# First readers of loaded data pinned to their place, logits turned ahead of rows, two experts' weights spread over the last batch, and the overflow loop moved behind the last scatter

## The chip, the cores and the metric

The kernel runs on one core of a Trainium2 chip. The metric is device time in microseconds (us), the median of three runs. TensorE (PE) multiplies, VectorE (DVE) and ScalarE (ACT) work on tiles, GpSimd (POOL) issues the indirect DMAs, and SyncE (SP) issues the other DMAs.

## The reference

Squared-ReLU attention over 8 batches of 1856 rows, gated by `u`, and then a mixture of 16 experts (4 groups of 4) in which each of the 14,848 rows goes to one expert:

```python
scores = (1.0 / S) * np.matmul(z, z.transpose(0, 2, 1))
attn = np.maximum(scores, 0.0) ** 2
x = (u * np.matmul(attn, v)).reshape(B * S, D)       # D = 256
g_idx = np.argmax(x @ w_group, axis=1)               # 4 groups
...                                                  # g_w: softmax weight of the group
e_idx = np.argmax(xg @ w_expert[g], axis=1)          # 4 experts in the group, e_w likewise
h = np.maximum(xg[mask_e] @ w1[g, e], 0.0)           # 256 -> 1024
out[tok_idx] = (g_w * e_w)[:, None] * (h @ w2[g, e]) # 1024 -> 256
```

## The kernel before

**Attention.** Each batch is cut into four chunks of 512, 512, 416 and 416 query rows (c0 to c3), and each chunk into 15 key blocks: 480 steps, named (c, k) within a batch. A step issues the scores of the step five ahead (`scores(s + LEAD)`: two matmuls, a ReLU and a square on ACT, a high half `ah` and a low half `al` on DVE), and then six matmuls into the output (`attn_v`). Numbers are kept as a high and a low half in fp32r, so every operand that is loaded is split once: ACT copies the high half from the staging tile, and DVE subtracts to get the low half. These are the first readers of loaded data: `z2h` (L229), `vh` (L296), `w1h` (L173) and `w2` (L185).

**Routing.** After the last key block of a chunk, `chunk_end` makes `xT`. `planes` (ACT, L386) lays out its 16-bit planes, and four DMA transposes on SP (L392) turn them into rows. `logits` runs four matmuls (L400, L401), copies the result (ACT, L405), and one more DMA transpose on SP (L408) brings it to `lgx`; `logits_tr` (DVE, L414) is the first reader of `lgx`. Then `route` runs some 26 small DVE operations, three per step, and four indirect DMAs on POOL (L535) scatter the rows into one bucket per expert in DRAM.

**Order.** From step 15 to 479 the order on each engine is made by a planner. It simulates the program with a cost model and puts an instruction where its inputs are ready by that model; program order only decides between those that are ready. Each engine then runs its list strictly in order and waits at the head of it. The first 15 steps, and the whole expert stage (PE, ACT and DVE there), are in an order written by hand. `defer(s + n, ...)` sets after which step a piece is put into the program, `run_gens` advances `route`.

**The last batch (batch 7).** When the rows of batches 0 to 6 are counted, the experts are sorted by load. `fill` (POOL, L616) writes padding rows behind each expert's rows, 16 DMAs of 396 KB. The first expert's weights are loaded in four 512 KB pieces (`load_w`, L169 and L178) and split. The first 512 rows of the two fullest experts are already final; `load_rows(0)` and `load_rows(1)` fetch them, and `join_block` (L685 to L700) makes the operands of block 0.

**Experts.** 16 experts, most in two blocks of up to 512 rows; a block has eight steps g, each with six `up` and six `down` matmuls. The last chunk's deferred pieces and its `route` run in the first steps g. Results are turned back by DMA transposes (L760) and scattered to the output by POOL (L731). The last block's results come by `rows_down` without a transpose. At the end a loop (L1147) handles overflowing experts; with this data it runs no iteration.

Of the kernel before, what the change touches and what calls it, by code (L numbers as in the profile page):

```python
# [29 lines left out]
def tile_glu_attn_moe(  # L30
# [133 lines left out]

    def load_w(e, wt, piece, name):

        raw = new_stg(f"raw_{name}_{piece}")
        if piece < 2:
            nc.sync.dma_start(raw, w1[ds(e, 1), piece * P:(piece + 1) * P, :].rearrange("o p f -> p (o f)"))  # L169

            def split():
                hi, lo = wt["h"][piece], wt["l"][piece]
                nc.scalar.copy(out=hi, in_=raw)  # L173
                nc.vector.tensor_sub(out=lo, in0=raw, in1=f32(hi))
        else:
# [6 lines left out]
            def split():  # L182
                for j in range(2):
                    t = wt["2"][2 * q + j].rearrange("p (a t d) -> p a t d", a=2, t=2)
                    nc.scalar.copy(out=t[:, :, 0, :], in_=rv[:, 2 * j:2 * j + 2, :])  # L185
                    nc.vector.tensor_sub(out=t[:, :, 1, :], in0=rv[:, 2 * j:2 * j + 2, :], in1=f32(t[:, :, 0, :]))
# [3 lines left out]
    def new_w(name):  # L190
        h, l = [], []
        for d in range(ND):
            h.append(new_vb(f"w1h_{name}_{d}"))
            l.append(new_vb(f"w1l_{name}_{d}"))
        return {"h": h, "l": l, "2": [new_vb(f"w2_{name}_{q}") for q in range(4)]}
# [21 lines left out]
    def prep_z(b, c):  # L217
# [8 lines left out]
        def split():  # L226
            z2h = new_z(f"z2h_{b}_{c}")
            z2l = new_z(f"z2l_{b}_{c}")
            nc.scalar.copy(out=z2h[:, 0:wx], in_=zr[:, 0:wx])  # L229
# [49 lines left out]
    def prep_v(b, c):  # L279
# [12 lines left out]
        def split():  # L292
# [3 lines left out]
            nc.scalar.copy(out=vh[:, 0:e], in_=raw[:, 0:e])  # L296
# [59 lines left out]
    def chunk_end(s):  # L356
# [24 lines left out]
        def planes(d):  # L381
# [8 lines left out]
            if d == ND - 1:  # L390
                for t in range(nt):
                    nc.sync.dma_start_transpose(  # L392
                        rows[:, t, 0:D].bitcast(U16).rearrange("p (g d) -> p g d", d=P),
                        pl[:, t].rearrange("p g q -> p (g q)"),
                    )

# [15 lines left out]
        def logits_tr():  # L412
            lgf = rt_("lgf", [4, LP], f"{b}_{c}")[:, 0:nt]
            nc.vector.tensor_copy(  # L414
                out=lgf.bitcast(U16).rearrange("p t (l h) -> p t h l", h=2)[:, :, :, 0:2 * NL], in_=lgx[:, :, :, 0:2 * NL]
            )
# [26 lines left out]
    def route(b, c, rows, lg, nt, part):  # L443
# [25 lines left out]
        yield  # L469
        oh = t("oh", [NG, 4])  # L470
        nc.vector.tensor_tensor(out=oh, in0=key, in1=km.unsqueeze(2).to_broadcast([P, NG, 4]), op=ALU.is_equal)
        yield
# [12 lines left out]
        yield  # L485
        pre = t("pre", [nt, NE], BF16)
        nc.vector.tensor_copy(out=pre[:, 0, :], in_=oh16[:, 0, :])
        yield
        for i in range(1, nt):
            nc.vector.tensor_add(out=pre[:, i, :], in0=pre[:, i - 1, :], in1=oh16[:, i, :])  # L490
            yield
        yield True
        for _ in range(3):
            yield
# [14 lines left out]
        yield  # L509
        df = t("df", [nt])  # L510
# [4 lines left out]
        yield  # L515
        nc.vector.tensor_add(out=base, in0=pk[:, W:W + NE], in1=base)
        yield
        sm = t("sm", [NG])
        nc.vector.tensor_reduce(out=sm, in_=ex, axis=AX.X, op=ALU.add)
        yield  # L520
        nc.vector.tensor_scalar(out=sm, in0=sm, scalar1=1e-9, scalar2=None, op0=ALU.add)
        yield
        nc.vector.reciprocal(out=sm, in_=sm)
        yield
        smv = sm.rearrange("p (i g) -> p i g", g=5)
        sel = t("sel", [nt, 4])
        nc.vector.tensor_mul(out=sel, in0=smv[:, :, 1:5], in1=ohv[:, :, 0, :])
        yield
        ew = t("ew", [nt])
        nc.vector.tensor_reduce(out=ew, in_=sel, axis=AX.X, op=ALU.add)  # L530
        yield
        nc.vector.tensor_mul(out=rows[:, 0:nt, D].bitcast(F32), in0=ew, in1=smv[:, :, 0])
# [269 lines left out]
    PE, ACT, DVE, SP = (mybir.EngineType.PE, mybir.EngineType.Activation, mybir.EngineType.DVE, mybir.EngineType.SP)  # L802
# [65 lines left out]
    )  # L868
    xs = []
    e1_cuts = []  # L870
    def step(s):
        b, c, k = steps[s]
        nxt = s // NK + 1
        if k == 0:
            if nxt < B * NQ:
                load_ut(nxt // NQ, nxt % NQ)
            if b + 1 == B:
                if c == 0:
                    new_wt(0)
                pw.clear()  # L880
                if c:
                    pw.append(load_w(regs(0)[0], wts[0], c - 1, "e0"))
                if c == NQ - 1:
                    pw.append(load_w(regs(0)[0], wts[0], c, "e0"))
        if b + 1 == B and k in (11, 13) and pw:
            pw.pop(0)()
        if s == NS - 1:
            new_wt(1)
            e1_cuts.extend([load_w(regs(1)[0], wts[1], pc, "e1") for pc in range(2)])
# [10 lines left out]
        if b + 1 == B and c == NQ - 1 and k == 4:  # L900
            for i in range(NEARLY):
                load_rows(i)
        if s == NS - 4:
            xs.append(list(join_block(0))[-1])
        if b + 1 == B and 0 <= s - (NS - NQ * NK + NK + 1) < NE:
            fill(s - (NS - NQ * NK + NK + 1))
# [8 lines left out]
    pw = []  # L915
# [15 lines left out]
    def early(i):  # L931
        run_deferred(late["at"])
        run_gens(late["at"], 8)
# [135 lines left out]
    def weights_from(g):  # L1069
        i = g // NF  # L1070
        if i == 0:
            ld, cuts, when = 1, e1_cuts, (1, 2, 6, 8)
        else:
            pe_ = blocks[i - 1][0]
            ld = pe_ + 2 if last_use[pe_] == i - 1 and pe_ + 2 < NE else None
            when = (4, 7, 10, 13)
            if ld is None:
                return
            new_wt(ld)
            cuts = [load_w(regs(ld)[0], wts[ld], pc, f"e{ld}") for pc in range(2)]  # L1080
# [6 lines left out]
        for pc in range(4):  # L1087
            then(g + when[pc], lambda pc=pc: piece(pc))

    def downs(g):  # L1090
# [5 lines left out]
        if f == NF - 1:  # L1096
            for k, fn in enumerate(turn(i, yb.pop(i), rows_b.pop(i)[1], n)):
                then(g + AHEAD + 5 + k, fn)

    plans = []  # L1100
    order = tc.manual_schedule(
        engines={mybir.EngineType.PE, mybir.EngineType.Activation, mybir.EngineType.DVE}
    )
    with order:
        for g in range(NB * NF):
# [28 lines left out]
            if i >= OLD:  # L1134
# [5 lines left out]
                if i == NB - 1 and f == NF - 1:  # L1140
# [65 lines left out]
```

## Time and profile before

| | us |
|---|---|
| median of 3 runs (lowest, highest) | 1563.68 (1561.2, 1564.03) |
| the profiled execution, its own time | 1563.37 |
| its span | 1561.8 |
| PE busy in the span | 1529.6 |
| DVE busy | 1131.8 |
| ACT busy | 1004.3 |
| POOL busy | 307.6 |

The 1.6 us between span and own time lie outside the profiled instructions. A matmul's end is modelled, so PE counts as busy a little beyond its last start. The mean granted clock of the span was 0.994.

### The profile page before, as it was taken

The page shows a single profiled execution, that of the slowest core. Times are in us where ns is not written, and L with a number is a line of the kernel's source. Part 1 is how long each engine was busy: PE and PEld are TensorE (multiplying, and loading weights), DVE is VectorE, ACT ScalarE, POOL GpSimd, SP SyncE. Part 2 cuts the span into 40 slices and gives each one's busy share as a digit, 9 for nine tenths or more (in the row PEclk, how much of TensorE's full clock was granted, in tenths as well). Part 3 has the DMA queues.
Part 4 walks back from the last instruction along what each step waited for, and adds up shares of the span by engine and source line. Part 5 has one row for each costly group of instructions (what it writes and reads, how often), then busy time and mean ns, then how long its engine had stood idle before and what let it go on. Part 6 is the DMA issues. An engine that isn't in the chain of part 4 may idle for free.

```text
span 1561.8 us, 23340 instructions
## 1 busy us (share of the span) xinstructions
PE 1529.6 (98%) x7527; PEld 1337.7 (86%) x7527; DVE 1131.8 (72%) x2676; ACT 1004.3 (64%) x1896; POOL 307.6 (20%) x372
## 2 busy tenths in 40 slices
PE   9999999999999899999989999999999999999996
PEld 7897988978979889889869799998888888888895
DVE  7888787887897788887877668765665555666662
ACT  8887797887897787978867435444444444444441
POOL 0013111212112121212142221211211122221112
PEclk9999999999999999999999999999999999999998
DMA  4344252342433332413184454554444544544530
GB/s 140 102 100 98 64 137 56 80 115 67 106 83 79 106 87 56 112 46 101 51 267 100 101 117 118 131 132 107 115 122 113 129 118 124 125 125 126 127 78 27
DMA packets 297388, 163.52 MB, mean 105 GB/s; under 512 B 240027, under 2 KB 276899, under 8 KB 297264
## 3 DMA queue, kind: packets, MB, share of 16 engines
q1 hardware_dynamic: 283168, 124.24, 33.5%
q0 software_dynamic: 13744, 37.39, 7.6%
q8 instruction: 59, 0.97, 0.3%
q14 instruction: 65, 0.53, 0.1%
q10 hardware_dynamic: 352, 0.39, 0.1%
HBM read 72.50 MB, written 38.45 MB: 71 GB/s over the span
## 4 chain that ended last, share of the span: by engine, by line
issue 32%; PE 26%; DVE 6%; DMA 5%; POOL 5%; ACT 3%; SPq 1%; POOLq 0%; DVEq 0%; ACTq 0%
PE o L345 5%; PE o L346 5%; PE o L348 4%; POOL out_dram L731 4%; PE sc L315 2%; PE sc L316 2%; DMA lgx<-lgp 2%; DVE al L328 2%; DMA out_dram<-yf,meta 2%; PE ph L712 1%; PE ph L710 1%; PE ph L711 1%; DVE ah L325 1%; DMA raw_e<-in_w_dram 1%; PE y L728 1%
## 5 line engine op out<-in xcount | busy, mean ns | idle before, releaser
L715 ACT ACTIVATE hh<-ph 128x512 fp32r<-128x512 f32 (+10 forms) x288 | 156.3, 543 | 349.8 <-PE ph L712 336.1
L345 PE MATMUL o<-ah,vl 128*128 128x416 f32 (+1 forms) x960 | 359.0, 374 | 2.8 <-DVE ah L325 1.7
L346 PE MATMUL o<-ah,vh 128*128 128x416 f32 (+1 forms) x960 | 356.4, 371 | 0.0
L716 DVE SCALAR_TENSOR_TENSOR hl<-ph,hh 128x512 fp32r<-128x512 f32 (+10 forms) x288 | 177.3, 616 | 217.8 <-ACT hh L715 200.9
L318 ACT ACTIVATE r<-sc 128x512 f32<-128x512 f32 (+1 forms) x480 | 259.6, 553 | 104.9 <-PE sc L316 50.4
L328 DVE TENSOR_TENSOR al<-r,ah 128x512 fp32r<-128x512 f32 (+1 forms) x448 | 285.6, 638 | 31.6 <-ACT r L322 16.1
L348 PE MATMUL o<-al,vh 128*128 128x512 f32 (+1 forms) x896 | 290.4, 375 | 11.6 <-DVE al L328 10.7
L324 ACT ACTIVATE r<-r 128x512 f32<-128x512 f32 (+1 forms) x416 | 240.3, 591 | 5.8
L535 POOL DMA_INDIRECT bucket<-rows,di x128 | 141.2, 1103 | 449.7 <-issue 197.9
L731 POOL DMA_INDIRECT out_dram<-yf,meta x121 | 122.7, 1014 | 508.5 <-DVE yf L770 484.4
L712 PE MATMUL ph<-xl_m,w1h_e 128*128 128x512 f32 (+10 forms) x576 | 207.9, 361 | 1.2 <-issue 0.8
L710 PE MATMUL ph<-xh_m,w1l_e 128*128 128x512 f32 (+10 forms) x576 | 207.5, 360 | 0.4 <-DVE hl L716 0.4
L711 PE MATMUL ph<-xh_m,w1h_e 128*128 128x512 f32 (+10 forms) x576 | 207.6, 360 | 0.0
L345 PEld LDWEIGHTS o<-ah,vl 128*128 128x128 f32 x960 | 181.3, 189 | 25.9 <-DVE ah L325 4.1
L348 PEld LDWEIGHTS o<-al,vh 128*128 128x128 f32 x896 | 166.2, 189 | 38.9 <-DVE al L328 20.4
L346 PEld LDWEIGHTS o<-ah,vh 128*128 128x128 f32 x960 | 181.2, 189 | 18.9
L728 PE MATMUL y<-hl,w_e 128*128 128x512 f32 (+9 forms) x544 | 196.2, 361 | 0.0
L727 PE MATMUL y<-hh,w_e 128*128 128x512 f32 (+9 forms) x544 | 196.1, 360 | 0.0
L726 PE MATMUL y<-hh,w_e 128*128 128x512 f32 (+9 forms) x544 | 195.9, 360 | 0.0
L325 DVE CAST ah<-r 128x512 fp32r<-128x512 f32 (+1 forms) x416 | 169.4, 409 | 34.2 <-ACT r L324 27.5
L315 PE MATMUL sc<-zm,z2h 128*128 128x512 f32 (+1 forms) x480 | 181.7, 379 | 1.1 <-ACT r L318 1.0
L316 PE MATMUL sc<-zm,z2l 128*128 128x512 f32 (+1 forms) x480 | 178.6, 372 | 0.0
(171 smaller groups left out, 2102.2 us busy)
## 6 DMA issues: line engine op xcount, KB each, us to landing
raw_e<-in_w_dram SPq DMA_DIRECT2D x64, 512.0 KB
vr<-in_v_dram SPq DMA_DIRECT2D x23, 512.0 KB
ut<-in_uT_dram SPq DMA_DIRECT2D x16, 512.0 KB
ut<-in_uT_dram SPq DMA_DIRECT2D x16, 416.0 KB
bucket<-padrow POOLq DMA_DIRECT2D x16, 396.0 KB
zr<-in_zT_dram SPq DMA_DIRECT2D x47, 128.0 KB
vr<-in_v_dram SPq DMA_DIRECT2D x9, 256.0 KB
rows<-pl SPq DMA_TRANSPOSE x128
```

The source lines that it names most:

```text
L315: nc.tensor.matmul(ps[:, 0:w], z2h[:, ks], zm, start=True, stop=False)
L316: nc.tensor.matmul(ps[:, 0:w], z2l[:, ks], zm, start=False, stop=True)
L318: nc.scalar.activation(out=a, in_=ps[:, 0:w], func=AF.Relu, scale=1.0 / S)
L324: nc.scalar.activation(out=a, in_=a, func=AF.Square)
L328: nc.vector.tensor_sub(out=al, in0=a, in1=f32(ah))
L345: nc.tensor.matmul(o, vl[:, dsl], ah, start=(k == 0), stop=False)
L346: nc.tensor.matmul(o, vh[:, dsl], ah, start=False, stop=(k == NK - 1))
L348: nc.tensor.matmul(o, vh[:, dsl], al, start=False, stop=False)
L710: nc.tensor.matmul(o, wt["l"][d][:, fs], xh[:, d, 0:W], start=(d == 0), stop=False)
L711: nc.tensor.matmul(o, wt["h"][d][:, fs], xh[:, d, 0:W], start=False, stop=False)
L712: nc.tensor.matmul(o, wt["h"][d][:, fs], xl[:, d, 0:W], start=False, stop=(d == ND - 1))
L728: nc.tensor.matmul(o, w2t[:, 0, dsl], hl_[:, 0:W], start=False, stop=(f == NF - 1))
```

## The change

- **Pins.** `held` ties an instruction behind whatever was put into the program before it on its engine, so that the planner can't move it ahead. It is used for the ACT copies that read loaded data first, for `logits_tr` on DVE, and for the four row transposes on SP.
- **Logits ahead of rows.** `logits` at step s + 2 now precedes `planes` at s + 3 and s + 4 (before: `planes` at s + 1 and s + 2, `logits` at s + 2). `logits_tr` comes at s + 6 instead of s + 8. For the last chunk it is the other way: `logits` at s + 5 (before s + 3), `logits_tr` at s + 8 (before s + 6), and `route` then runs up to 20 operations a step instead of 8.
- **Route.** The softmax weights are computed between the other operations, ahead of the scatter address.
- **Last batch.** The first expert's four weight pieces are loaded at (1,4), (1,5), (1,10), (1,14) and split at (1,9), (1,13), (2,5), (2,8); before, their loads were put at the starts of c1, c2 and c3. The second expert's pieces are loaded in c2 and c3, and three of them split there; before, all four were split in the expert stage. The fills go two per step from (1,5), instead of one per step from (1,1). `load_rows(0)` is at (2,3) and `load_rows(1)` at (3,4), before both at (3,4); block 0 is joined at (2,10) to (2,12), before at (3,11).
- **Expert stage.** SP is in hand order there too. Rows go out one step later.
- **The end.** The last block's `rows_down` and the overflow loop are in one hand order for all engines, POOL too, so the loop's instructions come behind the last scatter.

```diff
+    free = [True]
+
+    def held(ins):
+        if free:
+            tc.keep_in_program_order(ins)
...
-                nc.scalar.copy(out=hi, in_=raw)
+                held(nc.scalar.copy(out=hi, in_=raw))
...
-                    tr = nc.sync.dma_start_transpose(
+                    if s >= NHELD:
+                        held(tr)
...
-        defer(s + 1, lambda: planes(0))
-        defer(s + 2, lambda: planes(1))
-        defer(s + (3 if last else 2), logits)
-        wait = 6 if last else 8
+        defer(s + (5 if last else 2), logits)
+        defer(s + 3, lambda: planes(0))
+        defer(s + 4, lambda: planes(1))
+        wait = 8 if last else 6
         defer(s + wait, logits_tr)
-        gens.append((max(s + wait + 1, 42), g))
+        gens.append((s + wait if last else max(s + wait + 1, 42), g))
...
+    E0_LOADS = ((1, 4), (1, 5), (1, 10), (1, 14))
+    E0_CUTS = ((1, 9), (1, 13), (2, 5), (2, 8))
+    E1_LOADS = ((2, 9), (2, 13), (3, 7), (3, 11))
+    E1_CUTS = ((3, 6), (3, 9), (3, 13))
+    X0_LOADS = ((2, 3), (3, 4))
+    X0_JOINS = ((2, 10), (2, 11), (2, 12))
...
-        if b + 1 == B and 0 <= s - (NS - NQ * NK + NK + 1) < NE:
-            fill(s - (NS - NQ * NK + NK + 1))
+        if b + 1 == B and c == 1 and 5 <= k < 5 + NE // 2:
+            for e in range(2 * (k - 5), 2 * (k - 5) + 2):
+                fill(e)
...
-        run_gens(late["at"], 8)
+        run_gens(late["at"], 20)
...
-        engines={mybir.EngineType.PE, mybir.EngineType.Activation, mybir.EngineType.DVE}
+        engines={PE, ACT, DVE, SP}
...
+        with tc.manual_schedule(engines={POOL}):
+            for t in range((n + P - 1) // P):
+                rows_down(i, wts[e], hs, rows_b[i][1], n, t, next_view)
+            assert not hb
+            overflow()
```

## Rows read from the trace of the kernel before

**Rows 1.** The page, parts 1 and 2: busy time by engine, and the granted clock by slices.

```profile
PE 1529.6 (98%) x7527; PEld 1337.7 (86%) x7527; DVE 1131.8 (72%) x2676; ACT 1004.3 (64%) x1896; POOL 307.6 (20%) x372
PEclk9999999999999999999999999999999999999998
```

**Rows 2.** Waits of all engines (us in total, times, longest us).

```profile
DVE lgf L414 <- DMA lgx<-lgp: 62.6, 31, 5.0
...
PE o L348 <- DVE al L328: 10.7, 9, 4.0
...
ACT w1h_e L173 <- DMA raw_e<-in_w_dram: 5.9, 2, 4.4
...
ACT w_e L185 <- DMA raw_e<-in_w_dram: 2.9, 1, 2.9
```

**Rows 3.** Stretches: busy PE, PEld, DVE, ACT, POOL, then PEclk, DMA share, GB/s.

```profile
120.00:140.00 20.00, 17.95 (x72) 13.36 (x71) 14.86 (x50) 14.04 (x28) 6.54 (x9) 0.91 0.63 113
320.00:340.00 20.00, 18.68 (x83) 14.64 (x84) 19.34 (x55) 17.63 (x35) 2.91 (x4) 1.00 0.51 139
530.00:550.00 20.00, 15.17 (x61) 13.03 (x62) 17.41 (x49) 13.93 (x27) 0.64 (x2) 0.83 0.45 115
700.00:750.00 50.00, 50.00 (x266) 47.66 (x265) 40.38 (x122) 41.37 (x86) 9.41 (x13) 1.00 0.31 81
790.00:830.00 40.00, 35.45 (x164) 28.97 (x163) 28.93 (x79) 27.17 (x53) 13.14 (x20) 1.00 0.73 231
815.00:862.00 47.00, 44.42 (x227) 40.31 (x226) 37.14 (x115) 33.73 (x70) 10.18 (x13) 1.00 0.41 105
850.00:870.00 20.00, 17.66 (x83) 14.39 (x82) 16.02 (x46) 10.67 (x20) 4.67 (x6) 1.00 0.54 133
900.00:910.00 10.00, 9.22 (x46) 7.91 (x45) 6.28 (x10) 4.25 (x8) 4.35 (x4) 1.00 0.34 83
950.00:1500.00 550.00, 550.00 (x2720) 481.64 (x2719) 346.27 (x531) 252.75 (x453) 105.44 (x110) 1.00 0.49 122
```

**Rows 4.** Timeline of DVE from 126.6 us (start, us, what).

```profile
130.09 0.46 DVE L414 COPY lgf<-lgx 128x320 uint16<-128x320 uint16 x1 [3.42 <-DMA lgx<-lgp]
```

**Rows 5.** Timeline of SP and DVE ahead of 530 us.

```profile
523.95 0.57 SPq L284 DMA_DIRECT2D vr<-in_v_dram  x1
...
524.63 1.19 SPq L408 DMA_TRANSPOSE lgx<-lgp  x1
```

**Rows 6.** Timeline of all engines from 530.7 us.

```profile
530.76 0.35 DVE L414 COPY lgf<-lgx 128x320 uint16<-128x320 uint16 x1 [5.03 <-DMA lgx<-lgp]
...
533.82 0.71 PE L348 MATMUL o<-al,vh 128*128 128x416 f32 x1 [4.02 <-DVE al L328]
```

**Rows 7.** Timeline of PE from 529.3 us.

```profile
529.41 0.39 PE L316 MATMUL sc<-zm,z2l 128*128 128x512 f32 x1
```

**Rows 8.** The chain of waits, 785 to 815 us (start, us, what).

```profile
787.11 4.33 DMA raw_e<-in_w_dram
...
797.51 11.67 DMA raw_e<-in_w_dram
```

**Rows 9.** Line L616, the fills: min/median/max ns, first and last start.

```profile
L616 POOL DMA_DIRECT2D bucket<-padrow x16: 727/727/798, 778.6 to 806.3; - x16
```

**Rows 10.** Groups on DVE, 780 to 905 us (busy, mean ns, idle before).

```profile
L186 DVE TENSOR_TENSOR w_e<-raw_e,w_e 128x512 fp32r<-128x512 f32 x8 | 5.3, 686 | 1.5 <-ACT w_e L185 1.5
L174 DVE TENSOR_TENSOR w1l_e<-raw_e,w1h_e 128x1024 fp32r<-128x1024 f32 x4 | 4.9, 1224 | 3.3 <-ACT w1h_e L173 2.9 <-issue 0.4
...
L465 DVE TENSOR_TENSOR key<-key,iota 128x80 f32<-128x80 f32 x4 | 1.0, 240 | 0.1
```

**Rows 11.** Timeline of all engines from 1550.3 us.

```profile
1550.34 0.48 DVE L794 SCALAR_TENSOR_TENSOR y<-py,meta,tm 96x256 f32<-96x256 f32 x1 [2.33 <-ACT tm L793]
1553.11 0.92 POOL L731 DMA_INDIRECT out_dram<-y,meta  x1 [3.84 <-issue]
```

**Rows 12.** Line L1202, the end of the program.

```profile
L1202 POOLq DRAIN  x3: 40/115/8015, 1552.9 to 1561.5; - x3
```

More of the change, by code (lines that the diff above doesn't have):

```diff
@@ L190, in new_w, with add_w @@
     def new_w(name):
[L191 to L195, printed above, removed]
+        wt = {"h": [], "l": [], "2": []}
+        for piece in range(4):
+            add_w(wt, piece, name)
+        return wt
+    def add_w(wt, piece, name):
+        if piece < 2:
+            wt["h"].append(new_vb(f"w1h_{name}_{piece}"))
+            wt["l"].append(new_vb(f"w1l_{name}_{piece}"))
+        else:
+            wt["2"] += [new_vb(f"w2_{name}_{2 * (piece - 2) + j}") for j in range(2)]
     def new_wt(e):
@@ L491, in route @@
             yield
+            if i == 1:
+                sel = t("sel", [nt, 4])
+                nc.vector.tensor_mul(out=sel, in0=smv[:, :, 1:5], in1=ohv[:, :, 0, :])
+                yield
+            elif i == 2:
+                ew = t("ew", [nt])
+                nc.vector.tensor_reduce(out=ew, in_=sel, axis=AX.X, op=ALU.add)
+                yield
+        nc.vector.tensor_mul(out=rows[:, 0:nt, D].bitcast(F32), in0=ew, in1=smv[:, :, 0])
         yield True
-        for _ in range(3):
-            yield
+        yield
         pk = bank(ps_m, "m", f"pk_{b}_{c}")
@@ L800, in next_view @@
         return oviews[ocnt[0] - 1]
-    PE, ACT, DVE, SP = (mybir.EngineType.PE, mybir.EngineType.Activation, mybir.EngineType.DVE, mybir.EngineType.SP)
+    PE, ACT, DVE, SP, POOL = (
+        mybir.EngineType.PE, mybir.EngineType.Activation, mybir.EngineType.DVE, mybir.EngineType.SP, mybir.EngineType.Pool
+    )
     def first_batch():
@@ L879, in step @@
                     new_wt(0)
[L880 to L889, printed above, removed]
+        if b + 1 == B:
+            if (c, k) in E0_LOADS:
+                e0_cuts.append(load_w(regs(0)[0], wts[0], E0_LOADS.index((c, k)), "e0"))
+            if (c, k) in E0_CUTS:
+                e0_cuts[E0_CUTS.index((c, k))]()
+            if (c, k) in E1_LOADS:
+                wts.setdefault(1, {"h": [], "l": [], "2": []})
+                e1_cuts.append(load_w(regs(1)[0], wts[1], E1_LOADS.index((c, k)), "e1"))
+            if (c, k) in E1_CUTS:
+                pc = E1_CUTS.index((c, k))
+                add_w(wts[1], pc, "e1")
+                e1_cuts[pc]()
+            if (c, k) in X0_LOADS:
+                load_rows(X0_LOADS.index((c, k)))
+            if (c, k) == X0_JOINS[0]:
+                x0.append(join_block(0))
+            if (c, k) in X0_JOINS:
+                xs[:] = [next(x0[0])]
         if b + 1 < B:
@@ L1071, in weights_from, with last_piece @@
         if i == 0:
[L1072 to L1080, printed above, removed]
+            def last_piece():
+                add_w(wts[1], 3, "e1")
+                e1_cuts[3]()
+            then(g + 5, last_piece)
+            return
+        pe_ = blocks[i - 1][0]
+        ld = pe_ + 2 if last_use[pe_] == i - 1 and pe_ + 2 < NE else None
+        if ld is None:
+            return
+        new_wt(ld)
+        cuts = [load_w(regs(ld)[0], wts[ld], pc, f"e{ld}") for pc in range(2)]
         def piece(pc):
@@ L1087, in weights_from @@
         for pc in range(4):
-            then(g + when[pc], lambda pc=pc: piece(pc))
+            then(g + (4, 7, 10, 13)[pc], lambda pc=pc: piece(pc))
     def downs(g):
```

109 lines of the change are left out of this document (49 added, 60 removed).

## The prediction, made before the changed kernel was run

> **What bounds the kernel now.** The page comes first: PE is busy for 1529.6 of 1561.8 us [rows 1]. So PE sets the time, and only two things can be gained: what PE stands idle or runs at the lower clock, and what lies behind its last matmul. The view of stretches comes next, to find where PE stands. In the expert stage there is nothing: from 950 to 1500 us PE is busy for 550 of 550 us [rows 3]. The losses sit in six short stretches. In attention they are 120 to 140 us (17.95 of 20 busy), 320 to 340 (18.68) and 530 to 550 (15.17); around the last batch they are 790 to 830 (35.45 of 40), 850 to 870 (17.66 of 20) and 900 to 910 (9.22 of 10) [rows 3]. Idle time adds up to 2.05 + 1.32 + 4.83 = 8.2 us in the first three and 4.55 + 2.34 + 0.78 = 7.7 us in the last three. In two of them the granted clock is down as well, 0.91 and 0.83 [rows 3]: PE stood still, and then ran for some microseconds at the lower of its levels.
>
> The view of waits tells who is late. PE waits for `al` of DVE (10.7 us in 9 waits). DVE in turn waits 62.6 us in 31 waits for `lgx`, the transposed logits, and ACT waits 5.9 + 2.9 us for weights [rows 2]. The timeline joins the two. At 530.76 DVE begins to read `lgx` after 5.03 us of standing, and the `al` behind it releases PE at 533.82, after 4.02 us [rows 6]; PE's last start before was at 529.41 [rows 7]. The planner had put the reader where its model has `lgx` landed, and DVE's list is strictly in order. Most of the 31 waits cost PE nothing, because DVE works ahead; the 3.42 us wait at 130.09 [rows 4] and the 5.03 us one outlast that lead.
>
> **The change part by part.**
>
> *Logits first, reader pinned.* Before, four row transposes were put on SP's list ahead of that of the logits, and a `v` load could stand there too: the one at 523.95 preceded the logits' transpose at 524.63, which landed only by 530.76 [rows 5, 6]. Now the four come behind, and the reader can't stand ahead of the DVE work of step s + 11 (it is put into the program after `scores(s + 6 + LEAD)`). DVE can be at most those five steps ahead of PE, so the reader runs no earlier than six steps after the chunk's end. A step of 416 columns is 8 matmuls; 266 of them took 50 us from 700 to 750 [rows 3], so a step is 1.5 us and the place at least 9 us behind, later if DVE has less lead. I expect most of the 62.6 us of waits to go. What they cost PE in batches 0 to 6 is 8.2 us idle, plus the clock: (1 - 0.91) x 20 = 1.8 us, and (1 - 0.83) x 20 = 3.4 us, of which I count 2.0, since part of that low clock fell into the idle time. That is 12.0 us. A load may still stand ahead of a logits transpose, as the one at 523.95 did, so I take 80%: **-9.6 us**. Bounds: 0 (the reader is early again) and -13.
>
> *Hidden idle.* At 533.82 the page's idle is 4.02 us, but from 529.41 to 533.82 are 4.41 us between starts, and a 416-column matmul needs 0.19 (50 / 266): 0.2 us more was lost than the idle time shows. With some two dozen gaps in the six stretches I take **-2.5 us**, bounds 0 and -5.
>
> *Last batch.* The chain of waits shows one weight load landing in 4.33 us and the one at 797.51 in 11.67 us [rows 8]; the 16 fills run from 778.6 to 806.3 us [rows 9], and ACT stood behind those loads. Now each split is 5, 8, 10 and 9 steps behind its load: at 1.8 us a step in c1 the shortest is 9 us, the others 13 us or more, over the 11.67 us. The first load goes out a step before the fills, so it should land like the 4.33 us one. `load_rows(0)` and the join of block 0 move a chunk earlier, away from the wait for `xp` and the last logits. Against this, three more pieces are split in c3: a w1 piece costs DVE 1.22 us, a w2 piece twice 0.69 us [rows 10], together 3.8 us. DVE was busy for 37.14 of 47 us from 815 to 862 [rows 3], so it rises to 40.9, which is 92% of the 44.4 us that PE worked there. That just fits, not without small waits. Of 7.7 us I take 75%: **-5.8 us**, bounds -1 and -7.7.
>
> One page speaks against this part. The row: 11.67 us for a weight load beside the fills, 231 GB/s as a mean over that stretch [rows 3, 8]. The Trainium skill, page "DMA: Bandwidth & Descriptors", section "Issuing engines are not separate DMA queues", says that DMAs issued by different engines end up on the same 16 DMA engines and interleave; the trace agrees. By that rule the loads at (1,4) and (1,5), with the fills from (1,5), still share: should the first take 11.67 us, ACT would stand for 11.67 - 9 = 2.7 us at its split, and the sum would be some 2 us worse.
>
> *Last chunk's route.* `logits`, `logits_tr` and `route` stand two steps g later, but up to 20 operations go at once. A small DVE operation costs 0.24 us [rows 10], so 17 of them are a burst of 4 us, and the position matmuls that follow stand on PE's list behind it. **+1.0 us**, bounds 0 and +2.5.
>
> *SP by hand in the expert stage: 0.* SP's list waits there for ACT and DVE work of the same step g, and a weight piece is split at least three steps (8 us) after its load is put in. The cover is PE's 550 of 550 us. If it went, each block start could lose what 900 to 910 lost, 0.78 us [rows 3]. `route`'s reorder and the other pins: the same instructions, hidden behind PE in attention: 0.
>
> *The end.* The last `y` is written at 1550.82, its scatter starts only at 1553.11 [rows 11], because the loop's instructions stand ahead of it on POOL. That scatter can be 2.0 us earlier, but the loop's instructions now come behind it, and POOL's closing drain, which began at 1552.9, took 8.0 us [rows 12]. If the drain counts from the scatter: -2.0. If it counts from its own start: POOL stood 3.84 us between its last two scatters [rows 11], and those instructions come on top, some +1 to +3 us. No row decides; I take **0**, bounds -2 and +3.
>
> Sum: -9.6 - 2.5 - 5.8 + 1.0 + 0 = -16.9 us. Against the profiled execution's 1563.4 us (the median of the runs is 1563.7, so the same within 0.3) that is **1547 us**.
>
> **The rivals.**
>
> *Last batch bound by DVE and ACT.* If 92% of DVE can't be kept in order, c2 and c3 lose what they gain: 1547 + 4 = 1551. For: 40.38 of 50 is the fullest steady stretch of attention without loss [rows 3]. Against: the other batches' `v` and `z` splits are absent.
>
> *Half given back.* Pins fix a few instructions; the planner orders the rest anew, and the gaps return elsewhere: 1547 + 8 = 1555.
>
> *The pins change nothing for `lgx`.* With a load ahead on SP the transposed logits still land behind the pinned place, and only the last batch gains: 1547 + 9.6 = 1557.
>
> *Slower: the pinned reader is early in chunk after chunk.* A pin can't be moved back by the planner. The 3.42 us wait cost PE 2.05 us idle and 1.8 us of clock in its stretch [rows 3, 4], some 3.8 us. If seven more chunks of the 32 do that, the gain on the logits is gone and 27 us come on top: 1557 + 27 = 1584. It decides from about two more chunks on. Against: the place is at least 9 us behind, and SP no longer has the rows first.
>
> **How the numbers follow.** The forecast has 0.54, the last batch bound 0.14, half given back 0.12, no gain on `lgx` 0.09, the slower case 0.09, and 0.02 remain for a larger gain. A change under 0.2% (3 us) can't be told from none. Of the 0.09 without gain on `lgx` I give 0.04 to no change, and 0.01 of the half given back. Faster: 0.86, no change 0.05, slower 0.09. The low end takes the better bounds of the logits, hidden idle and the end together (-3.4 - 2.5 - 2, and the last batch in full): 1547 - 10 = 1537, with a little room 1536; the high end takes in the third rival with the end's +3: 1560.
>
> **What would show it.** `lgx` waits on DVE fall from 62.6 us to below 15, and ACT's waits for weights to zero. The dips of the granted clock near 130 and 530 us vanish. PE's idle time from 120 to 910 us falls below 6 us. The last scatter starts right behind the last `y`. Wrong: new waits of DVE or ACT right at the pinned readers, or PE waits in c2 and c3 of the last batch.

## Result, and the profile after

The changed kernel takes 1541.8 us, the median of four runs (1540.96 to 1543.94), against 1563.48 us beside it (1561.2 to 1564.03): a ratio of 0.9866, with a 95% interval of 0.9849 to 0.9883. It is faster, by 5 us more than forecast and inside the range. Executions of one kernel differ by some us, so two medians 2 to 3 us apart are only told apart where their intervals are. The profiled execution has an own time of 1542.55 us and a span of 1540.9 us.

The page first: PE's busy time, and the head of the chain that ended last (the work that led to the end, followed back step by step). It runs mostly through matmuls.

```profile
PE 1518.9 (99%) x7527; PEld 1336.9 (87%) x7527; DVE 1117.9 (73%) x2676; ACT 1000.0 (65%) x1896; POOL 307.6 (20%) x372
...
PE 48%; issue 3%; DVE 2%; DMA 2%; ACT 1%; SPq 1%; POOL 1%; POOLq 0%; DVEq 0%; ACTq 0%
```

The waits of all engines (us in total, times, longest) answer to [rows 2]: `lgx` costs DVE 18.4 us instead of 62.6, PE's waits for `al` have gone from 10.7 us to 0.4, and ACT's two waits for weights are as long as they were.

```profile
DVE lgf L428 <- DMA lgx<-lgp: 18.4, 13, 3.0
...
ACT w1h_e L179 <- DMA raw_e<-in_w_dram: 5.9, 1, 5.9
...
ACT w_e L191 <- DMA raw_e<-in_w_dram: 3.0, 1, 3.0
...
PE o L360 <- DVE al L340: 0.4, 1, 0.4
```

The same stretches as in [rows 3], and 15 to 700 us, which is batches 0 to 6 but for their edges; there the kernel before has PE busy for 675.00 us, with 3214 matmuls. All three dips of attention are gone, 20.00 of 20 at a clock of 1.00. Around the last batch a loss remains, and 790 to 830 us has a lower clock than before.

```profile
15.00:700.00 685.00, 684.60 (x3315) 602.60 (x3314) 566.08 (x1605) 573.35 (x1102) 124.30 (x150) 1.00 0.35 91
120.00:140.00 20.00, 20.00 (x93) 16.22 (x92) 17.81 (x52) 15.47 (x29) 6.46 (x8) 1.00 0.40 108
320.00:340.00 20.00, 20.00 (x92) 16.24 (x91) 15.80 (x40) 16.77 (x33) 4.90 (x5) 1.00 0.40 107
530.00:550.00 20.00, 20.00 (x91) 16.54 (x91) 16.91 (x49) 16.48 (x30) 4.66 (x5) 1.00 0.31 81
790.00:830.00 40.00, 37.38 (x187) 34.43 (x188) 33.15 (x95) 34.29 (x71) 7.06 (x11) 0.96 0.50 154
815.00:862.00 47.00, 45.30 (x219) 38.73 (x218) 40.02 (x120) 29.78 (x62) 10.96 (x12) 1.00 0.53 122
850.00:870.00 20.00, 19.24 (x87) 15.51 (x86) 12.31 (x39) 10.60 (x20) 8.21 (x8) 1.00 0.40 81
900.00:910.00 10.00, 10.00 (x68) 10.00 (x67) 7.42 (x16) 4.47 (x11) 4.15 (x4) 1.00 0.35 93
```

Where the time came from is read from three marks in the timelines: the first `xT` of batch 0's third chunk (88.73 us before, 88.77 after), the first `xT` of batch 6's last chunk, and the last `y`. The second mark, before and then after:

```profile
750.07 1.08 DVE L366 TENSOR_TENSOR xT<-o,ut 128x416 f32<-128x416 f32 x2
```

```profile
730.78 0.58 DVE L378 TENSOR_TENSOR xT<-o,ut 128x416 f32<-128x416 f32 x1
```

So batches 0 to 6 gave 19.3 us. The last `y` ends at 1528.95 instead of 1550.82 [rows 11], 21.9 us earlier, so the last batch and the experts gave 2.6 in these two executions. From there to the end of the span are 12.0 us instead of 10.9, which takes about 1 back (all timelines count from the span's start).

The view of stretches between the first two marks, before and then after, holds the same work but for four matmuls. PE's idle time falls from 10.00 to 0.40 us, which is half of the gain; the other half is busy time, 651.34 against 641.61.

```profile
88.73:750.07 661.34, 651.34 (x3132) 568.91 (x3131) 540.12 (x1548) 537.50 (x1039) 130.52 (x155) 0.99 0.36 88
```

```profile
88.77:730.78 642.01, 641.61 (x3128) 567.06 (x3127) 528.73 (x1544) 533.41 (x1039) 128.77 (x155) 1.00 0.35 90
```

How a turned logits transpose now looks, from the timelines of SP and DVE in batch 1, at the place of [rows 4]: it goes out at 121.56, the four row transposes behind it, and `lgf` reads at 125.33 without any wait.

```profile
121.56 1.21 SPq L422 DMA_TRANSPOSE lgx<-lgp  x1
123.36 5.29 SPq L404 DMA_TRANSPOSE rows<-pl  x4
...
125.33 0.35 DVE L428 COPY lgf<-lgx 128x320 uint16<-128x320 uint16 x1
```

What remains in the last batch is in the chain of waits from 770 us. Four row transposes take 2.58 to 3.23 us each (without the fills beside them 1.28, below), the load of the first expert's second piece stands behind them on SP until 782.77, and then takes 7.27 us to land.

```profile
770.73 2.58 SPq L404
...
773.36 2.91 SPq L404
...
776.32 2.97 SPq L404
...
779.34 3.23 SPq L404 DMA_TRANSPOSE rows<-pl  x1
...
782.77 7.27 DMA raw_e<-in_w_dram
```

The timelines of ACT and PE show what that costs: ACT's split, pinned ahead of the next ReLU, stands 5.92 us, PE stands 3.26 us for that ReLU, and behind it matmuls of 416 columns appear with 0.55 us instead of 0.35.

```profile
790.07 1.04 ACT L179 CAST w1h_e<-raw_e 128x1024 fp32r<-128x1024 f32 x1 [5.92 <-DMA raw_e<-in_w_dram]
...
791.59 0.45 PE L327 MATMUL sc<-zm,z2h 128*128 128x416 f32 x1 [3.26 <-ACT r L330]
...
792.44 0.35 PE L357 MATMUL o<-ah,vl 128*128 128x416 f32 x1
792.63 0.55 PE L327 MATMUL sc<-zm,z2h 128*128 128x416 f32 x1
```

The last chunk's `route`: PE waits at its position matmuls (`pk`), 0.21 + 0.53 us.

```profile
861.35 0.20 PE L529 MATMUL pk<-oh,tri 128*128 128x64 bf16 x1 [0.21 <-DVE oh L503]
862.08 0.18 PE L530 MATMUL pk<-pre,ones 128*128 128x48 bf16 x1 [0.53 <-DVE pre L512]
```

The end: the last scatter starts 0.28 us behind the last `y`, and POOL's closing drain (the third number is the longest, in ns) begins at 1533.2 and lasts 6.85 us.

```profile
1528.47 0.48 DVE L808 SCALAR_TENSOR_TENSOR y<-py,meta,tm 96x256 f32<-96x256 f32 x1 [2.33 <-ACT tm L807]
1529.23 0.92 POOL L745 DMA_INDIRECT out_dram<-y,meta  x1 [1.83 <-DVE y L808]
...
L1239 POOLq DRAIN  x3: 40/109/6854, 1533.2 to 1540.7; - x3
```

### The profile page after: what moved, and what is told of

Its sections match the earlier page's. It is cut to its first block, busy times and chain, and to the rows that moved or that the text cites. A ratio compares the mean times of both kernels' runs of the same rounds, so it can differ in the third digit from the quotient of the medians.

```text
span 1540.9 us, 23215 instructions
## 1 busy us (share of the span) xinstructions
PE 1518.9 (99%) x7527; PEld 1336.9 (87%) x7527; DVE 1117.9 (73%) x2676; ACT 1000.0 (65%) x1896; POOL 307.6 (20%) x372
## 4 chain that ended last, share of the span: by engine, by line
PE 48%; issue 3%; DVE 2%; DMA 2%; ACT 1%; SPq 1%; POOL 1%; POOLq 0%; DVEq 0%; ACTq 0%
PE ph L726 7%; PE ph L725 7%; PE ph L724 7%; PE y L742 6%; PE y L741 6%; PE y L740 6%; PE o L357 2%; PE o L358 2%; PE o L360 2%; PE sc L327 1%; PE sc L328 1%; PE py L802 1%; DMA raw_e<-in_w_dram 1%; SPq L404 1%; POOL out_dram L745 0%
## 5 line engine op out<-in xcount | busy, mean ns | idle before, releaser
L357 PE MATMUL o<-ah,vl 128*128 128x512 f32 (+1 forms) x960 | 357.0, 373 | 1.6 <-DVE ah L337 1.4
L358 PE MATMUL o<-ah,vh 128*128 128x512 f32 (+1 forms) x960 | 356.7, 372 | 0.0
L360 PE MATMUL o<-al,vh 128*128 128x512 f32 (+1 forms) x896 | 281.0, 373 | 0.4 <-DVE al L340 0.4
```

Source lines behind the costliest of these rows:

```text
L357: nc.tensor.matmul(o, vl[:, dsl], ah, start=(k == 0), stop=False)
L358: nc.tensor.matmul(o, vh[:, dsl], ah, start=False, stop=(k == NK - 1))
L360: nc.tensor.matmul(o, vh[:, dsl], al, start=False, stop=False)
```

## The experiments

Theory: batches 0 to 6 gained because DVE no longer begins to read `lgx` before it has landed. Two parts of the change could do that, the order on SP (logits ahead of rows) and the pin of the reader, and the rivals are that one of them alone carries it. For the last batch the theory is that the new stall at 791.59 us ate the gain, by its place on SP or by the fills beside it. For the end, that the drain counts from POOL's own last work.

The table holds what the marks give in one profiled execution of each kernel: A from batch 0's third chunk to batch 6's last (their first `xT`), B from there to the end of the last `y`, C from there to the end of the span, and, from all executions, the median and the ratio to the kernel before on the same chip.

| run | A | B | C | median us | ratio (95%) |
|---|---|---|---|---|---|
| before | 661.3 | 800.8 | 10.9 | 1563.48 | 1 |
| changed | 642.0 | 798.2 | 12.0 | 1541.8 | 0.9866 (0.9849 to 0.9883) |
| logits first in the program, on before | 654.6 | 804.9 | 10.9 | 1562.87 | 1.0001 (0.9991 to 1.001) |
| reader's pin alone, on before | 644.8 | 803.2 | 10.9 | 1552.78 | 0.9952 (0.9935 to 0.9969) |
| changed, no pins | 659.0 | 798.4 | 12.0 | 1556.56 | 0.9958 (0.9941 to 0.9974) |
| changed, rows pinned alone | 659.6 | 799.8 | 12.0 | 1561.34 | 0.9992 (0.9978 to 1.0005) |
| changed, reader pinned alone | 643.6 | 805.5 | 12.0 | 1550.9 | 0.9917 (0.9901 to 0.9934) |
| changed, rows and reader pinned | 644.1 | 801.3 | 12.0 | 1546.92 | 0.9891 (0.9875 to 0.9908) |
| changed, last batch as before | 641.2 | 797.3 | 12.0 | 1541.77 | 0.9868 (0.9852 to 0.9885) |
| changed, loop outside | 641.5 | 800.8 | 10.9 | 1541.5 | 0.9854 (0.9837 to 0.9871) |
| changed, two loads first | 641.7 | 801.3 | 12.0 | 1545.15 | 0.9865 (0.9842 to 0.9889) |
| changed, fills behind rows | 641.6 | 796.2 | 12.0 | 1539.41 | 0.9838 (0.9821 to 0.9854) |
| the same, loop outside | 641.3 | 797.3 | 10.9 | 1539.71 | 0.9858 (0.9841 to 0.9874) |
| the same, and route faster | 641.6 | 794.1 | 10.9 | 1537.89 | 0.9851 (0.9835 to 0.9867) |

A is steady: the changed kernel and the last six rows, which share its batches 0 to 6, lie between 641.2 and 642.0. B is not. "Changed" and "loop outside" are the same program up to the last `y`, and have 798.2 and 800.8: in the second execution the second piece's load took 9.60 us instead of 7.27, ACT stood 7.90 us for it, and PE 5.36 instead of 3.26 (the waits of "loop outside"):

```profile
ACT w1h_e L179 <- DMA raw_e<-in_w_dram: 7.9, 1, 7.9
...
PE sc L327 <- ACT r L330: 5.4, 1, 5.4
```

So a difference in B of 2 to 3 us between two of these rows shows nothing by itself.

**Logits first in the program, on the kernel before.**

```diff
-        defer(s + 1, lambda: planes(0))
-        defer(s + 2, lambda: planes(1))
-        defer(s + (3 if last else 2), logits)
+        if last:
+            defer(s + 1, lambda: planes(0))
+            defer(s + 2, lambda: planes(1))
+            defer(s + 3, logits)
+        else:
+            defer(s + 2, logits)
+            defer(s + 3, lambda: planes(0))
+            defer(s + 4, lambda: planes(1))
```

> The kernel before with one part of the change: the logits and their transpose are put ahead of the row planes and the row transposes (all chunks but the last), and nothing is pinned; the reader stays at s + 8 for the planner to place. Behind the kernel before, the stretches of batches 0 to 6 lost about 19 of the 21.7 us that the change gained. Theory (the late transpose was the fault: four row transposes of 1.25 us stood ahead of it on SP): the waits of DVE for lgx fall from 62.6 to below 25 us, and the time is 1547 to 1550 us. Rival (the early place of the reader was the fault, the pin cures it): the waits stay above 45 us and the time is 1559 to 1563 us.

Measured: no change, a ratio of 1.0001, and 59.1 us of `lgx` waits. The timelines of SP and DVE in batch 1 say why: program order only decides between what is ready, so three of the four row transposes still go out first, and DVE stands for `lgx` again. In the other 31 chunks all four still go first, by SP's timeline. The edit left the order on SP nearly as it was, so this run doesn't test the theory of the late transpose; the pin of the rows below does. In the profiled execution, the fastest of ten, A fell by 6.7 us and B rose by 4.1; where the 6.7 come from, with the order on SP unchanged, is open.

```profile
119.10 3.88 SPq L392 DMA_TRANSPOSE rows<-pl  x3
123.08 1.21 SPq L408 DMA_TRANSPOSE lgx<-lgp  x1
...
128.38 0.35 DVE L414 COPY lgf<-lgx 128x320 uint16<-128x320 uint16 x1 [3.52 <-DMA lgx<-lgp]
```

**No pins.**

```diff
-    free = [True]
+    free = []
```

> The changed kernel with no instruction pinned; everything else as changed, the reader at s + 6. If the order on SP carries the gain, the waits for lgx stay below 25 us and the time is 1541 to 1545 us. If the pins carry it, the planner moves readers ahead of their data again, waits for lgx rise above 40 us, and the time is 1555 to 1560 us. If the split of the first expert's second piece waited 5.9 us only because it is pinned, that wait goes and the last batch gains up to 5 us, which would show as a time below 1541 us.

Measured: 1556.56 us, 51.9 us of `lgx` waits, and A is back at 659.0. The pins carry batches 0 to 6. ACT still waits 3.8 us for the first expert's w1 pieces, at the first of their two splits, and the third guess, a time below 1541 us, is wrong as well.

**One pin group at a time.** In the first run only the row transposes are pinned, in the second only the reader, in the third both, with ACT's copies free. `loose` does nothing.

```diff
-                held(nc.scalar.copy(out=hi, in_=raw))
+                loose(nc.scalar.copy(out=hi, in_=raw))
...
-            held(nc.vector.tensor_copy(
+            loose(nc.vector.tensor_copy(
```

> The changed kernel in which only the four row transposes on SP are pinned; the reader of lgx on DVE and the ACT copies are free. The trace without pins shows three of the four row transposes ahead of that of the logits again (119.74 against 123.87 us), although the logits come first in the program, and 4.5 us of standing at 130 us. Theory (what counts is the place of the row transposes: pinned, they let the logits' transpose go out at once): the 51.9 us of lgx waits fall below 25 us and the time is 1541 to 1546 us. Rival (the reader's place counts; free, the planner puts it as early as its model allows): waits above 40 us, 1552 to 1557 us. If each carries part: about 1549 us.

> The changed kernel in which only the reader of lgx on DVE is pinned, behind the DVE work of step s + 11; the row transposes and the ACT copies are free. Theory (the place of the row transposes counts): they stand ahead of the logits' transpose again, the reader still waits, above 35 us in all, and the time is 1550 to 1557 us. Rival (the reader's place counts): six steps behind the chunk's end are enough even for a late transpose, the waits fall below 20 us, and the time is 1541 to 1546 us.

Measured: rows alone 1561.34 us, with 46.1 us of waits; reader alone 1550.9 us, with 4.0 us of waits. In the first run the logits do go ahead of the rows on SP, in all chunks but the first and the last, and still the free reader stands for them; A is 659.6, only 1.7 us below the kernel before (timelines of SP and DVE in batch 1):

```profile
122.91 1.23 SPq L425 DMA_TRANSPOSE lgx<-lgp  x1
124.32 5.89 SPq L407 DMA_TRANSPOSE rows<-pl  x4
...
126.95 0.35 DVE L431 COPY lgf<-lgx 128x320 uint16<-128x320 uint16 x1 [2.77 <-DMA lgx<-lgp]
```

The theory that I had put first, the place of the row transposes, falls; the rival holds for A, 643.6 against 642.0, though not for the time that it named. In the second run all four row transposes still stand ahead, the transpose goes out at 122.63, 1.1 us later than in the changed kernel, and the reader, held back to 129.20, waits for nothing (timelines of SP and DVE, then the view of waits):

```profile
117.37 5.16 SPq L407 DMA_TRANSPOSE rows<-pl  x4
122.63 1.73 SPq L425 DMA_TRANSPOSE lgx<-lgp  x1
...
129.20 0.35 DVE L431 COPY lgf<-lgx 128x320 uint16<-128x320 uint16 x1
...
DVE lgf L431 <- DMA lgx<-lgp: 4.0, 7, 1.0
```

Its time is still 9 us above the changed kernel, of which A is 1.6 and B 7.3. Why B is longer here is not shown: without any pin it is 798.4.

> The changed kernel in which the row transposes on SP and the reader of lgx are pinned, and the ACT copies that read loaded data are free: the last of the pin groups by itself. So far: no pin 1556.6 us, rows alone 1561.3, reader alone 1550.9, all 1541.8. Theory (the ACT pins are what holds the first expert's second split at a place where its load is late; free, the planner moves it behind work that is ready): the 5.9 us wait of ACT shrinks below 3 us, the lgx waits stay below 20 us, and the time is 1537 to 1540 us. Rival (the planner's model has the weights landed early and moves the splits ahead, as it did the reader): ACT's waits for weights stay at 5 us or more in all, and the time is 1542 to 1548 us. If the reader's and the rows' pins together give all of batches 0 to 6, PE is busy for at least 684 of 685 us from 15 to 700 us in either case.

Measured: 1546.92 us, 5 us above the changed kernel, but the intervals of the ratios overlap, so what the pins of ACT's copies are worth in time is not settled. The rival holds: free, the first split comes where its load has not landed and waits 6.24 us, against 5.92 at the pinned second one. PE is busy for 683.14 of 685 us from 15 to 700 us, a little under the 684 expected.

**The reader's pin alone, on the kernel before.**

```diff
-            nc.vector.tensor_copy(
+            ins = nc.vector.tensor_copy(
...
+            if not last:
+                tc.keep_in_program_order(ins)
```

> The kernel before with one thing changed: the reader of lgx on DVE is pinned where it stands in the program, at s + 8, in all chunks but the last. Rows still come before the logits on SP. In the changed kernel with this pin alone the lgx waits were 4.0 us and PE was busy for 683.67 of 685 us from 15 to 700 us, against 675.00 before. Theory (the reader's place is the whole gain of batches 0 to 6, some 18 us, and the late transpose doesn't matter): lgx waits below 10 us, PE busy for at least 683 of 685 us, and, with the last batch as it was before or up to 5 us worse, 1545 to 1550 us. Rival (it needs the logits ahead of the rows as well): the pinned reader still waits, over 20 us in all, and the time is 1553 to 1560 us.

Measured: `lgx` waits of 8.0 us and PE busy for 684.49 of 685 us, as the theory has it: with all four rows first on SP in every chunk and nothing else changed, one pin gives A all but 2.7 us of its gain in this execution. The time is 1552.78 us, 9.3 us below the kernel before beside it, between the two: the profiled execution took 1548.52, the other three 1552.6 to 1556.6, with a mean clock of 0.993 or 0.994 against 0.996. Where those lose is not in a trace.

**The last batch as before.** Loads at the starts of c1 to c3, the second expert split in the expert stage, rows at (3,4), join at (3,11); fills, pins, logits, route and end as changed.

```diff
-            if (c, k) in E0_LOADS:
-                e0_cuts.append(load_w(regs(0)[0], wts[0], E0_LOADS.index((c, k)), "e0"))
...
+                if c:
+                    pw.append(load_w(regs(0)[0], wts[0], c - 1, "e0"))
...
+        if s == NS - 4:
+            xs.append(list(join_block(0))[-1])
```

> The changed kernel with the last batch's weights and the first block's rows where they were: loads at the starts of c1, c2, c3, the second expert split in the expert stage, rows of blocks 0 and 1 at (3,4), the join at (3,11). The fills stay two a step from (1,5), and pins, logits order, route and the end are as changed. If that part of the change is worth what was forecast, 5.8 us, the time is 1547 to 1548 us. If a new stall of PE at 791.6 us (3.4 us, and some 1.6 us at the lower clock behind it) took most of it, as the trace of the changed kernel suggests, it is worth 2 to 3 us and the time is 1544 to 1545 us. If the waits are caused by the fills alone, wherever the loads stand, it is worth nothing: 1542 us.

Measured: 1541.77 us. With the rest of the change in place, spreading weights and rows is worth nothing that the runs can tell (their intervals are some 2.7 us to either side). The third outcome named that time, but for another reason. There is no stall at 791 us here (790 to 830 is 40.00 of 40), but the timelines of DVE and PE show one at 834 us: `xf` waits for the block's rows, `oh` of the route stands behind it on DVE, and PE stands 3.50 us.

```profile
832.19 1.31 DVE L699 COPY xf<-xp 128x2048 uint16<-128x2048 uint16 x1 [2.61 <-DMA xp<-bucket]
...
834.03 0.20 PE L529 MATMUL pk<-oh,tri 128*128 128x64 bf16 x1 [3.50 <-DVE oh L503]
```

So the change does take this wait away, as intended for the join, and another of the same size stands 42 us ahead of it.

**Two loads first; fills behind the rows.** The first puts both w1 loads ahead of the row transposes on SP; the second lets the first fill wait for the last of those transposes.

```diff
-    E0_LOADS = ((1, 4), (1, 5), (1, 10), (1, 14))
+    E0_LOADS = ((1, 3), (1, 3), (1, 10), (1, 14))
```

```diff
+        if e == 0:
+            tc.add_manual_dep(
+                ins.ins, last_tr[0].ins.name,
...
+            )
```

> The changed kernel with the first two weight pieces of the first expert both loaded at (1,3), ahead of the four pinned row transposes on SP. In the changed kernel the second load is issued at 782.77 us, behind row transposes that took 11.84 us, and ACT's split stands 5.92 us for it. Theory (the place in SP's list is the fault): the load goes out near 769 us and is there long before its split near 784 us; the wait falls to 0, the stall of PE at 791.59 us (3.43 us and 1.6 us at the lower clock) goes, and the time is 1536 to 1538 us. Rival (the fills on the same DMA engines make the load slow wherever it stands): the load takes over 10 us, the wait stays above 2 us, and the time is 1540 to 1542 us.

> The changed kernel with the first of the 16 fills held until the last row transpose of the last batch's first chunk is done, so that the transposes run without the fills beside them. They took 2.6 to 3.2 us each beside the fills, and 6.3 us for four, 1.6 us each, a chunk earlier. Theory (the fills share the DMA engines with SP's transfers and slow them): the four transposes take 5 to 7 us, the second load goes out near 777 us, the split's wait falls from 5.9 to at most 2 us, and the time is 1537 to 1539 us. Rival (only the place on SP counts, the transposes are slow for another reason): they still take over 10 us, and the time is 1541 to 1543 us. A third outcome: the later fills now meet the loads themselves, the wait moves to the third piece, and the time stays at 1541 us.

Measured: loads first 1545.15 us, which is no gain; three of its four runs are at 1545, one at 1538.9. The second piece is there in time, as the place in SP's list would have it, but the third, issued at 784.18 among the fills, takes 19.93 us, and ACT waits 7.05 us at its split instead (the chain of waits, then ACT's timeline).

```profile
784.18 19.93 DMA raw_e<-in_w_dram
...
804.13 1.14 ACT L191 CAST w_e<-raw_e 128x512 fp32r<-128x512 f32 x2 [7.05 <-DMA raw_e<-in_w_dram]
```

With the fills behind the rows the time is 1539.41 us, 0.9838 (0.9821 to 0.9854). The timeline of SP has the four row transposes in 5.12 us and the second load out at 775.64, and of ACT's waits for weights 0.5 us is left. Both outcomes point to the fills: what SP moves beside them is slow, and its place in the list decides which transfer that is. The wait at the second piece needs both, the late place and the fills: taking away either ends it.

```profile
770.32 5.12 SPq L404 DMA_TRANSPOSE rows<-pl  x4
775.64 0.42 SPq L175 DMA_DIRECT2D raw_e<-in_w_dram  x1
```

The median is only 2.4 us below that of the changed kernel, and the intervals still touch (0.9849 to 0.9883 there), so the gain in time isn't shown. PE now stands at 846.12 us: the last chunk's logits need the bank of PSUM (the memory that matmuls write to) of the route before, which DVE frees with `base` (timelines of DVE and PE).

```profile
845.81 0.17 DVE L541 TENSOR_TENSOR base<-pk,base 128x16 f32<-128x16 f32 x1
846.12 0.43 PE L415 MATMUL pl<-xh,whl 128*128 128x416 f32 x1 [3.02 <-DVE base L541]
```

**The loop outside.**

```diff
-        with tc.manual_schedule(engines={POOL}):
-            for t in range((n + P - 1) // P):
-                rows_down(i, wts[e], hs, rows_b[i][1], n, t, next_view)
-            assert not hb
-            overflow()
+        for t in range((n + P - 1) // P):
+            rows_down(i, wts[e], hs, rows_b[i][1], n, t, next_view)
+        assert not hb
+    overflow()
```

> The changed kernel with the overflow loop outside the hand order again, as before: its instructions on POOL stand ahead of the last scatter. From the last y to the end of the span are 11.0 us before and 12.0 us after. Theory (POOL's closing drain takes some 6.9 us from whichever comes last, POOL's own last work or the last scatter's end; with the loop behind the scatter its instructions come on top): 1540.8 us, 1.0 us faster than the changed kernel. Rival (the scatter is what the drain waits for, and the early scatter pays): 1543 to 1544 us. Either way the difference is close to what the rounds can tell; the stretch from the last y to the end of the span decides.

> The changed kernel with the fills held behind the row transposes and the overflow loop back outside the hand order. From the last y to the end of the span were 12.0 us in every trace with the loop behind the scatter and 11.0 us in every one with it ahead. Theory: the two add up, 1539.4 - 1.0 = 1538.4 us, and the stretch from the last y to the end of the span is 11.0 us. Rival: the end gives nothing that the time shows, 1539.4 us.

Measured: C is 10.9 us in both, as in the other four traces with the loop ahead of the last scatter, and 12.0 us in all eight with the loop behind it. The times, 1541.5 against 1541.8 and 1539.71 against 1539.41, can't tell 1 us. The end of the second kernel by the timelines of DVE and POOL and the line that closes the program: the scatter starts 2.3 us behind the end of the last `y` instead of 0.28, and still the drain ends at 1529.3 + 8.0 = 1537.3, 10.0 us behind that `y`; in the changed kernel it ends 11.1 us behind it (1533.2 + 6.85 - 1528.95).

```profile
1526.78 0.48 DVE L816 SCALAR_TENSOR_TENSOR y<-py,meta,tm 96x256 f32<-96x256 f32 x1 [2.33 <-ACT tm L815]
1529.54 0.92 POOL L753 DMA_INDIRECT out_dram<-y,meta  x1 [3.83 <-issue]
...
L1246 POOLq DRAIN  x3: 40/115/8009, 1529.3 to 1537.9; - x3
```

**Route of the chunk before, faster.** On top of the last kernel.

```diff
-        run_gens(s, 3)
+        run_gens(s, 6 if s >= NS - NK else 3)
```

> As the run before it, and in the last chunk's steps the route of the chunk before advances six operations a step instead of three. With the fills held, PE stood 3.18 us at 846.12 us: the last chunk's logits matmul needs the PSUM bank that the previous chunk's position counts fill until DVE reads them for base at 845.81 us. Theory (that route is late, and it holds the bank): its small operations end 2 to 4 us earlier, the stall goes, and the time is 1535 to 1536.5 us. Rival (DVE is so full in this stretch that six operations a step only push al and ah back, and PE stands at those instead): 1538 to 1540 us.

Measured: 1537.89 us, with an interval that overlaps that of the run before it. The mechanism that was expected did not come about: the logits' matmul still waits 3.2 us for `base`, at 845.3 us. The lowest median of the study is this one; that it is better than the version with the fills alone is not shown, and by the ratios that version is the lower one (0.9838 against 0.9851).

## Why the prediction was right, and where it was off

| step | forecast | measured |
|---|---|---|
| batches 0 to 6 (logits and reader -9.6, hidden idle -2.5) | -12.1 | -19.3 |
| last batch -5.8, last chunk's route +1.0, SP by hand 0 | -4.8 | -2.6 |
| the end | 0 | +1.0 |
| sum | -16.9 | -20.9 |

**Logits first, reader pinned.** The mechanism was right: the reader stood too early on DVE's list, and the place behind step s + 11 is late enough, without a wait in A that costs PE anything. Of the two causes that the step named, the runs leave one. With the reader pinned and the rows first, A falls by 17.8 of the 19.3 us (16.6 on the kernel before); with the logits first on SP and the reader free, by 1.7, and the time doesn't move (0.9992). The slower rival, a pinned reader that is early in chunk after chunk, stays away, and so does the one in which a load ahead on SP undoes the pin: even four row transposes ahead don't.

**Its size** is the step that failed: -12.1 forecast, -19.3 measured. The 80% was too careful, since 0.4 us of idle time is left in 685. And the loss had been read from three dips, as 8.2 us of idle time and 3.8 of clock, with 2.5 more for what idle time doesn't show. Between the marks idle time fell by 10.00 - 0.40 = 9.6 us, and the busy time of the same work by 651.34 - 641.61 = 9.7 us, which no idle time shows; I had 3.8 + 2.5 = 6.3 for that. The lower clock that the rows show in the two dips accounts for at most 1.8 + 3.4 = 5.2 of the 9.7 [rows 3]; the other 4.5 or more, for which 2.5 was forecast, is near the step's bound of 5, and where it sits is not shown. A count of matmuls over a long stretch, against that of a stretch without loss and of the same steps, would have shown the size.

**Last batch.** The -5.8 was put on spreading weights and rows, and that step failed too: the run without it is as fast (1541.77 us). The forecast said that the first load goes out a step before the fills. It didn't, though it was in time for its split (timelines of POOL and SP):

```profile
767.81 2.56 POOL L630 DMA_DIRECT2D bucket<-padrow  x3
768.78 0.39 SPq L175 DMA_DIRECT2D raw_e<-in_w_dram  x1
```

And the second load stood behind four row transposes, which that step of the working left out: it compared steps between load and split, and not what stands ahead on SP. The row is the 5.92 us wait. The rule of the Trainium skill, page "DMA: Bandwidth & Descriptors", section "Issuing engines are not separate DMA queues", that DMAs from different engines interleave on the same 16 DMA engines, was given with a stand of 2.7 us and a sum 2 us worse; the trace agrees in kind, with 5.92 us, but at the second piece, and with the transposes slowed as well as the load. The run with the fills held back shows it: the transposes fall from 11.84 to 5.12 us. That the sum for these steps came out 2.2 us worse is no test of it, since B differs by 2.6 between "changed" and "loop outside", which are the same program there. For the same reason it isn't shown that the -2.6 is more than that spread, and where it would come from is open. It isn't the spread of weights and rows, since the run without it has a B of 797.3; the run without pins has 798.4. What those share with the changed kernel, the fills two a step from (1,5), the later logits of the last chunk and SP's hand order, was not tried alone.

**The last chunk's route** was forecast at +1.0; PE's waits at its position matmuls are 0.74 us, about the size that was meant.

**The end** was put at 0 between two readings. The drain counts from POOL's own last work: it ends 6.9 us after it, whether that is the scatter (1552.9 + 8.0 - 1554.03 [rows 11, 12]) or the loop (6.85). So the loop's instructions behind the scatter come on top, at the low end of the +1 to +3 that was given for this reading.

**What was to be seen.** The dips are gone and the last scatter starts right behind the last `y`: right. The `lgx` waits are 18.4 us and not below 15, at no cost to PE. PE's idle time from 120 to 910 us is 790 - 783.97 = 6.0 us, at the bound named. ACT's waits for weights, 8.9 us, did not move: that sign of the last batch was wrong, and the sign that had been given for an error, a new wait right at a pinned reader, is the 5.92 us one.

**How much of it was luck.** The total was off by 4.0 us because two misses offset each other: batches 0 to 6 gave 7.2 us more than forecast, the last batch and the end 3.2 us less. The first is a right mechanism with its size too small; the -5.8 of the second is a step that the runs do not bear out.

## What to carry to other kernels

Where a planner with a cost model sets the order, look for the first readers of DMA results and pin them behind enough work; here one pinned instruction per chunk gave 16.6 of the 19.3 us in batches 0 to 6, and the order of the transfers, which seemed to be the cause, 1.7. The whole kernel with that pin alone gained only 9.3 us in its median, so look at the rest of the program again after such a pin. Check in the trace that an edit of the order did change it: putting the logits first in the program did not. When loads are moved, write down what stands ahead of each on its queue and what else moves at that time: beside the bulk fills transposes took more than twice as long and one weight load 19.93 us, so fills are better put where no one waits. And size a loss on the bounding engine by how many instructions it finished between two marks, because idle time showed only half of it (9.6 of 19.3 us).

## What the hardware did that was not expected

A row transpose of 1.28 us took 2.6 to 3.2 us beside the fills. Of the 512 KB weight loads that went out among them, w1 pieces took 4.33 [rows 8], 7.27 and 9.60 us, the last two the same load in two executions; w2 pieces took 11.67 [rows 8] and 19.93. A plan that counts on the shortest fails. POOL's closing drain took 6.9 us from POOL's last work in both arrangements (the scatter's end or the loop's instructions), so starting the scatter 2 us sooner didn't end the program sooner.
